# Top-k attention and an exact-GELU MLP on one core: more of P transposed by the vector engine and DRAM, with single buffers elsewhere to make room

## The chip, the cores and the metric

The kernel runs on one core of one Trainium2 chip, as one launch. The metric is the device time of the kernel in microseconds; lower is better. The engines are named as in the profile: PE (matmuls and transposes through the array; PEld is its weight loads), DVE (vector), ACT (scalar, activations), POOL (general) and SP, which only issues DMAs here. Each engine executes its own instructions strictly in the order of the program; what ties engines together are waits on semaphores.

## The reference

```python
B, H, S, D = 8, 8, 576, 64                       # q, k, v: (B, H, S, D)
scores = matmul(q, k.T) / sqrt(D)
kth = 32nd largest of each row
scores = where(scores >= kth, scores, -1e9)
attn = exp(scores - max); attn /= attn.sum(-1) + 1e-9
x = matmul(attn, v)  ->  (B * S, H * D) = (4608, 512)
h = x @ w_in                                      # (512, 2048)
out = (0.5 * h * (1 + erf(h / sqrt(2)))) @ w_out  # (2048, 512)
```

All is float32.

## The kernel before

**Items.** Two heads of a batch are a pair, four pairs a batch. The 576 rows of a head are 4 times 128 (`NM`, main rows) and 64 last rows. An item is a tile of scores of 128 partitions by 2 x 576: a main item has 128 rows of both heads of a pair, a last item the 64 last rows of the four heads of two pairs. There are 144 items, 18 to a batch; an even batch has its two last items behind the main ones, an odd batch ahead of them, so that four last items stand together (16 to 19, 52 to 55, 88 to 91, 124 to 127). 36 items, two batches, are a period of everything that follows.

**Slots.** One pass of the main loop is called slot n here. It is a software pipeline written out by hand: the loop issues, in this order and to every engine's queue, the work of slot n, and nothing reorders it later. In slot n:

- scores of item n+2 (in even slots also of n+3) are made by PE and copied by ACT into a tile `s` (L386, L394; `bufs=6`);
- the P of item n-2 is transposed, because the product with v needs the keys on the partitions (`transposes`). Either PE does it, with eight transposes into `tp` (L649), one or two of the 64 keys at the end (`tp_t`, L619, L622), and ACT copies them to `pt` (L664, L629, for last items `pt_end`, L635); or the item is *squared*: DVE transposes all 32x32 squares of `s` (`square_p`, L569), SP writes it to DRAM (`write_p`, L579, four DMAs) and reads it back into `pt` with the squares in their places (`read_p`, L586, four DMAs, one slot later). Before the change the squared items are 48 even main items from item 28 on;
- the product of P and v (`attend`, L715; last items L726) is made for item n-3, for main items once for two of them; ACT copies it into `xT`;
- select (Prelu against the 32nd value, L517) and exp (L529) of item n-1 run on ACT; the sum of exp goes to POOL (`add_small`, L510), the reciprocal to DVE (`inverse`, L504), and POOL multiplies the tile by it (`normalise`, L552);
- the top 32 of item n are found on DVE by MAX8 and MATCH_REPLACE8 (`top_k`, L483, L486), first on the pairwise maxima of the two halves of a row, whose sums POOL makes and splits (`sum_up` L447, `smaller` L455). `top_k` calls `middle` (the square of item n-2) ahead of its third round and `last` (the reciprocal of item n-1) at its end. `threshold` (L497, L498, POOL) then gives select its operands;
- pieces of the MLP fill PE (`mlp`, with a fixed number per slot from `room_in`).

**The MLP** goes by blocks of 256 tokens. In even slots PE makes pieces of the first product (`h_ps`, L773), which ACT passes through Gelu (L789) at the start of the odd slot; in odd slots it makes the second product in a form with seven products for eight (`second_block`): `seven_piece` (L927) and six `trio_piece`s (L929) that accumulate in three banks. In order of its pieces, an odd slot is one last piece of h, `seven`, then the others. A block takes four such odd slots. The first `seven` of a block is copied by ACT into a tile `y7` (L945), those of the other three are copied to `p7` (L948) and added to it by POOL (L950). When a block ends, ACT copies the banks out and POOL makes the four quarters of y from them: five sums (L979 to L983), then `lower` (L990), the last reader of `y7`, and `upper` (L994). POOL's sums are put in a list, `small`, from which `run_small` takes a few at the end of each slot, behind `normalise` and `sum_up`. Between blocks lie, once in a ring of 1152 tokens, 128 last tokens in a plainer form (`even_piece`); the very first block is plain too.

**PSUM** has eight banks: three for the second product, two each under the tags `pr` (scores, `tp`) and `l1` (h; in even slots also the second scores), and one, `z`, that the key scores (`last_keys`, `t_ps` or `tp_t`), the tails, `seven` and the product `o` take in turns. Whoever writes `z` next must wait until ACT has copied out what stands there.

**DMA.** SP issues nearly all of them in order. `load` brings q and k of a later pair for DVE to transpose by squares, with eight DMAs for each (four of 512 rows, four of the 64 last rows); calls that go through `issue` are held back in slots whose item n-2 is squared, until that item's write is issued.

## Time and profile before

| | |
|---|---|
| runs of the kernel before | 1480.89, 1480.30, 1479.78 us; median 1480.3 |
| the profiled execution, its own time | 1479.73 us |
| span of its instructions | 1478.0 us |
| busy, share of the span | PE 99%, DVE 88%, POOL 77%, ACT 74% |
| DMA, mean | 76 GB/s; queue q1 35.3% of 16 engines |

The span runs from the first to the last instruction that was profiled; the time of the execution has 1.7 us around it. In a row of a group stand the line, the engine, the operation, the tiles (out<-in), partitions and elements, the count, and then the busy time in us, the mean of one in ns, and the idle time ahead of it with what ended it. In a row of a timeline stand the start and the length in us, then the same names with the count of equal instructions merged. A float32 product shows as two rows of matmul for one instruction of the program, a transpose as one. Names drop the numbers of buffers, so `y` in `y<-seven` is the tile `y7`.

### The profile page before, as it was taken

Reading aid. Unit: us, or ns where it says so; the run is one execution under the profiler, and the core shown is the slowest. Engines: PE = TensorE matmul, PEld = TensorE weight load, DVE = VectorE, ACT = ScalarE, POOL = GpSimd, SP = SyncE. Lnnn points to the kernel's source line nnn. Section 1 sums busy time; section 2 is a strip of 40 time slices with the busy share of each in tenths; the row PEclk is TensorE's granted clock in tenths of the full one; section 3 lists DMA queues with packets and bytes.
Section 4 is the critical chain, followed back from the end, with each engine's and each line's share of the span. In section 5 each row is a group of like instructions: output and inputs, shape, how many; then the busy total and the mean of one; then the engine's idle time right before and its main releaser. Section 6 shows DMA issues by size and latency. Waiting matters only on the chain. (4 is left out here: it accounts for less than half of the span.)

```text
span 1478.0 us, 27006 instructions
## 1 busy us (share of the span) xinstructions
PE 1461.6 (99%) x8817; PEld 1147.9 (78%) x8817; DVE 1294.3 (88%) x3318; ACT 1099.9 (74%) x1942; POOL 1140.1 (77%) x1291
## 2 busy tenths in 40 slices
PE   8999999999999999999999999999999999999999
PEld 6876677877777777887777778787777777787787
DVE  8999899999999988999999987999999997998701
ACT  7999977877777687777777778777777777776620
POOL 6877567877898879877898978886788887987732
PEclk9999999999999999999999999999999999999999
DMA  7424310045435322345534331345453421233300
GB/s 198 143 86 124 84 48 1 24 88 101 95 73 93 66 58 52 65 95 108 105 83 81 69 61 47 66 93 99 97 103 73 89 55 41 61 61 72 70 15 15
DMA packets 477645, 112.94 MB, mean 76 GB/s; under 512 B 413216, under 2 KB 469056, under 8 KB 477504
## 3 DMA queue, kind: packets, MB, share of 16 engines
q1 hardware_dynamic: 476240, 110.78, 35.3%
q8 instruction: 70, 1.15, 0.3%
q14 instruction: 71, 0.58, 0.1%
q10 hardware_dynamic: 1200, 0.39, 0.1%
q0 software_dynamic: 64, 0.03, 0.0%
HBM read 73.39 MB, written 37.75 MB: 75 GB/s over the span
## 5 line engine op out<-in xcount | busy, mean ns | idle before, releaser
L773 PE MATMUL h_ps<-xT,w_in_sb 128*128 128x256 f32 (+1 forms) x2560 | 536.2, 361 | 0.1
L773 PEld LDWEIGHTS h_ps<-xT,w_in_sb 128*128 128x128 f32 x2560 | 436.5, 190 | 73.4 <-issue 25.2
L483 DVE MAX8 top<-lists 128x8 f32<-128x576 f32 (+1 forms) x792 | 476.4, 641 | 0.0
L486 DVE MATCH_REPLACE8 lists<-top,lists 128x288 f32<-128x288 f32 (+1 forms) x528 | 307.9, 589 | 0.0
L552 POOL TENSOR_TENSOR s<-s,rden 128x1152 f32<-128x1152 f32 x135 | 285.8, 2117 | 0.3 <-DVE rden L504 0.3
L529 ACT ACTIVATE s<-s,bias 128x576 f32<-128x576 f32 x288 | 225.4, 787 | 11.0 <-issue 0.4
L517 ACT ACTIVATE s<-s,neg 128x576 f32<-128x576 f32 x288 | 225.5, 793 | 1.7 <-POOL neg L497 1.6
L510 POOL TENSOR_SCALAR den<-den 128x2 f32<-128x2 f32 x144 | 31.4, 218 | 215.9 <-ACT s L529 210.2
L455 POOL TENSOR_TENSOR lists<-lists 128x576 int32<-128x576 int32 x132 | 186.2, 1410 | 4.0
L447 POOL TENSOR_TENSOR lists<-s 128x576 int32<-128x576 int32 x133 | 187.2, 1407 | 0.0
L715 PE MATMUL o<-pt,raw_v 128*64 128x256 f32 x1280 | 153.0, 384 | 1.8 <-ACT s L529 1.1
L715 PEld LDWEIGHTS o<-pt,raw_v 128*64 128x64 f32 x1280 | 87.8, 136 | 85.8 <-issue 37.2
L789 ACT ACTIVATE g<-h_ps 128x512 f32<-128x512 f32 x144 | 78.2, 594 | 100.6 <-PE h_ps L773 100.4
L929 PE MATMUL y_ps<-w_out_sb,sum 128*128 128x256 f32 x472 | 140.4, 379 | 0.0
L394 ACT ACTIVATE s<-s_ps 128x1024 f32<-128x1024 f32 x127 | 125.5, 1035 | 10.5 <-PE s_ps L386 10.3
L664 ACT COPY pt<-tp 128x1024 f32<-128x1024 f32 x85 | 86.6, 1019 | 62.2 <-PE tp L649 62.1
L386 PE MATMUL s_ps<-kt,qm 64*128 64x512 f32 x512 | 129.4, 618 | 0.8 <-ACT s L392 0.8
L504 DVE RECIPROCAL rden<-den 128x2 f32<-128x2 f32 x144 | 23.2, 161 | 108.6 <-POOL den L510 107.4
L486 DVE MATCH_REPLACE8 lists<-first,lists 128x288 f32<-128x288 f32 x264 | 114.3, 439 | 0.0
L929 PE MATMUL y_ps<-w_out_sb,g 128*128 128x256 f32 x480 | 113.4, 379 | 0.0
L483 DVE MAX8 first<-lists 128x8 f32<-128x288 f32 x268 | 106.6, 436 | 0.0
L929 PEld LDWEIGHTS y_ps<-w_out_sb,g 128*128 128x128 f32 x480 | 91.2, 190 | 12.4
(167 smaller groups left out, 2533.1 us busy)
## 6 DMA issues: line engine op xcount, KB each, us to landing
turned<-s SPq DMA_DIRECT2D x192, 144.0 KB, 3.5
pt<-turned SPq DMA_DIRECT2D x192, 144.0 KB, 3.2
raw_v<-in_v_dram SPq DMA_DIRECT2D x64, 128.0 KB, 2.4
out_dram<-y SPq DMA_DIRECT2D x30, 256.0 KB, 2.1
raw_q<-in_q_dram SPq DMA_DIRECT2D x112, 64.0 KB, 2.0
raw_k<-in_k_dram SPq DMA_DIRECT2D x112, 64.0 KB, 2.0
w_out_sb<-in_moe_w_in_dram SPq DMA_DIRECT2D x14, 511.8 KB, 4.8
w_out_sb<-in_moe_w_out_dram SPq DMA_DIRECT2D x10, 511.8 KB, 4.1
```

The costliest lines, as they stand in the source:

```text
L386: nc.tensor.matmul(s_ps[:, e], lhsT=q_t[rows, :], rhs=kt[rows, 0:SM], start=True, stop=True)
L394: nc.scalar.activation(spread(s, S + TL, SM), s_ps, func=AF.Copy, scale=scale)
L447: nc.gpsimd.tensor_tensor(t[:, :, 1].bitcast(i32), a.bitcast(i32), b.bitcast(i32), op=ALU.add)
L455: nc.gpsimd.tensor_tensor(into_of(i)[:, :, 1].bitcast(i32), both, top, op=ALU.subtract)
L483: nc.vector.max(x[:, e], src[:, e])
L486: nc.vector.match_replace(dst[:, e], x[:, e], src[:, e], LOWEST)
L517: nc.scalar.activation(s, s, func=AF.Prelu, bias=st["neg"][:, e : e + 1], scale=1.0, alpha=STEEP)
L529: nc.scalar.activation(s, s, func=AF.Exp, bias=st["bias"][:, e : e + 1], scale=1.0, accum_out=st["den"][:, e : e + 1],)
L552: nc.gpsimd.tensor_tensor(s, s, wide, op=ALU.mult)
L715: nc.tensor.matmul(o[e * D : (e + 1) * D, 0:n], lhsT=vt[:, j, e, :], rhs=pt[:, e * NJ + j if j < NM else NM, :], start=(j == 0), stop=(j = ...
L773: nc.tensor.matmul(h_tile(u)[:, i, :], lhsT=w_in_sb[:, ko, f * P : (f + 1) * P], rhs=xT[:, ko, c0 : c0 + n], start=(ko == 0), stop=(ko == ...
L929: nc.tensor.matmul(acc[names][:, k], lhsT=lhsT, rhs=rhs, start=(j == 0 and k == 0), stop=(j == FT // 2 - 1 and k == 1),)
```

## The change

- `squared` also holds for last items (from item 52 on) and for odd main items whose number in the period is 3, 13, 21, 25 or 29. Four last and five odd items of a period are added: 28 in all, 12 and 16.
- The last items get the layout of main items (keys of the second head turned round), so that they are squared and read into `pt` like those; `pt_end` goes.
- For the added odd items (`later`) the chain is moved forward: in the slot after theirs the reciprocal is taken ahead of the very last MAX8 (`early`) and `normalise` stands ahead of `threshold` on POOL; in the next the square follows the first MAX8s (`late`). Their product moves to the end of slot n+3. The products of delayed last items move too (`mid`: behind `seven` in an odd slot), and two MLP pieces move from a slot to the next where that next slot has no product at its usual place (`bare`).
- q and k of a pair come with four DMAs each, not eight, and through `issue`. The small loads of v behind delayed last items go to ACT's queue.
- Room in SBUF: seven tiles `s` instead of six; `part` has two buffers instead of three, `y7` one instead of two; p5 is kept in the half of `y1` that it ends in, and the sum is made in place.

```diff
-                    for at, lo, hi, by in ((0, 0, SM, queue), (SM + e * TL, SM, S, queue2)):
-                        by.dma_start(
...
+                    queue.dma_start(
+                        out=t[rows, at : at + S].rearrange("i (c j) -> i c j", j=SQ),
+                        in_=src[b, h0 + e, :, cols].rearrange("(c i) j -> i c j", i=SQ),
+                    )
...
-                load("q", pair + ahead)
+                issue(lambda: load("q", pair + ahead))
...
-        S_of[i] = s = work.tile([P, 2 * S], f32, tag="s", bufs=6, name="s")
+        S_of[i] = s = work.tile([P, 2 * S], f32, tag="s", bufs=7, name="s")
...
-    def top_k(i, last, middle):
+    def top_k(i, last, middle, early, late):
...
-            if 16 * r == TOPK:
+            if 16 * r == TOPK and not late:
                 middle()
             for e in range(2):
                 nc.vector.max(x[:, e], src[:, e])
+                if early and e == 0 and r == len(rounds) - 1:
+                    last()
+            if r == 0 and late:
+                middle()
...
-            if r == len(rounds) - 1:
+            if r == len(rounds) - 1 and not early:
                 last()
...
-        return SINGLE.stop - 2 < i < N - 2 and i % 2 == 0 and items[i][1] < NM and i % RINGS != 12
+        if not SINGLE.stop - 2 < i < N - 2:
+            return False
+        return items[i][1] == NM or (i % RINGS in LATER if i % 2 else i % RINGS != 12)
+
+    def later(i):
+
+        return i % 2 == 1 and squared(i) and items[i][1] < NM
+
+    def delayed(i):
+
+        return squared(i) and items[i][1] == NM
...
+    LATER = (3, 13, 21, 25, 29)
...
-                issue(lambda r=r: load("v", pair + r + NP))
+                issue(lambda r=r: load("v", pair + r + NP, None, nc.scalar if delayed(i) else None))
...
-        return work.tile([P, HALF], f32, tag="part", bufs=3, name="part")
+        return work.tile([P, HALF], f32, tag="part", bufs=2, name="part")
...
-            y7[0] = work.tile([P, HALF], f32, tag="y7", bufs=2, name="y7")
+            y7[0] = work.tile([P, HALF], f32, tag="y7", bufs=1, name="y7")
             nc.scalar.copy(out=y7[0], in_=seven[0][:, 0:HALF])
...
-            p2, p5, s7 = end_of["p2"], part_tile(), y7[0]
+            p2, p5, s7 = end_of["p2"], y1[:, B2], y7[0]
...
-            small.append((1, lambda: pool(y1[:, B2], s7, p5, op=add)))
             small.append((1, lambda: pool(y0[:, B2], y0[:, B2], p5, op=add)))
+            small.append((1, lambda: pool(p5, s7, p5, op=add)))
...
+    def bare(n):
+
+        return (n - 4 in starts and delayed(n - 4)) or later(n - 3)
...
-        return sizes[x] + (1 if x % 2 == 0 else -1)
+        return sizes[x] + (1 if x % 2 == 0 else -1) + 2 * (bare(n) - bare(n + 1))
...
-        read_p(n - 3)
+        mid = [i for i in (n - 5, n - 4) if delayed(i) and n % 2 and (i % 2 or i in starts)]
+        if not mid:
+            read_p(n - 3)
...
-        product = attend(n - 3)
+        if delayed(n - 4) and n % 2 == 0 and n - 4 not in starts:
+            product = attend(n - 4)
+        else:
+            product = not delayed(n - 3) and not later(n - 3) and attend(n - 3)
...
             softmax(n - 1, 0)
+            if mid:
+                for i in mid:
+                    attend(i)
+                copy_x()
+                read_p(n - 3)
             if n % 2:
                 mlp(ODD)
...
         run_gelus()
+        if later(n - 3):
+            attend(n - 3)
+            copy_x()
         if n < N:
-            top_k(n, lambda: inverse(n - 1), lambda: square_p(n - 2))
+            top_k(
+                n, lambda: inverse(n - 1), lambda: square_p(n - 2), later(n - 1), later(n - 2)
+            )
...
+        if later(n - 1):
+            normalise(n - 1)
         threshold(n)
...
-        normalise(n - 1)
+        if not later(n - 1):
+            normalise(n - 1)
```

## The prediction, as put on record before the changed kernel was run

> **What bounds the kernel now.** I read the page's head first, then the busy time by stretch, then the groups of the engine that fills its stretch.

> ```profile
> span 1478.0 us, 27006 instructions
> PE 1461.6 (99%) x8817; PEld 1147.9 (78%) x8817; DVE 1294.3 (88%) x3318; ACT 1099.9 (74%) x1942; POOL 1140.1 (77%) x1291
> ...
> core 0: us, PE busy (x) PEld busy (x) DVE busy (x) ACT busy (x) POOL busy (x), PEclk, DMA share, GB/s
> ...
> 703.60:1051.70 348.10, 347.59 (x2085) 273.54 (x2083) 321.92 (x832) 262.85 (x470) 286.62 (x323) 1.00 0.40 79
> ```

> The last row is one whole period of the schedule, two batches or 36 items (the window runs from the first MAX8 of item 72 to that of item 108). PE has work in 347.59 of its 348.10 us, DVE in 321.92. Busy PE alone would prove little, so I looked at the pace: the chain of waits shows runs of transposes and of products at a steady rate.

> ```profile
> 1279.34 0.87 PE tp L649 x8
> 1280.21 1.73 PE y_ps L929 x8
> ```

> Eight transposes take 0.87 us (0.109 each), eight passes of 256 columns 1.73 (0.216 each), one behind the other with no time between. So PE's own work sets the time: a microsecond of work less there is a microsecond less, and a microsecond in which PE waits is a microsecond more, because nothing after it has slack to make it up.

> **What the change takes away.**

> ```profile
> L649 PE MATMUL tp<-ident,s 128*128 128x128 f32 x696 | 90.4, 273 | 0.0
> L619 PE MATMUL tp_t<-ident,s 128*128 128x128 f32 x71 | 20.5, 288 | 1.6 <-POOL s L552 1.2
> L622 PE MATMUL tp_t<-ident,s 128*64 128x128 f32 x32 | 6.1, 273 | 0.0
> L664 ACT COPY pt<-tp 128x1024 f32<-128x1024 f32 x85 | 86.6, 1019 | 62.2 <-PE tp L649 62.1
> L569 DVE STREAM_TRANSPOSE s<-s 128x1152 f32<-128x1152 f32 x48 | 65.5, 1364 | 0.0
> ```

> The new `squared` holds 76 items where it held 48: 12 of the 16 last-row items and 16 odd main ones. These 28 lose eight transposes each, 28 x 0.87 = 24.4 us. Of the tails 16 (of L619) and 32 (L622) go and 4 come, 44 x 0.109 = 4.8. PE sheds 29.2 us, all of it on the path.

> DVE gains 28 x 1.364 = 38.2 us, nine squares or 12.3 us in a period: 321.92 + 12.3 = 334.2, against a PE period of 348.1 less 9.4 (nine items of 29.2 / 28), 338.7. DVE stays under PE, so I cost the squares at nothing; if the fit fails, the rival below prices it. ACT sheds 28 x 1.019 us of copies and takes 24 small loads of v onto its queue, which by a quarter of the read row below (2.54 / 4 = 0.64) are 15 us; ACT is busy in 262.85 of 348.10, so nothing. The halved q and k loads (4 DMAs, not 8) now stand behind a write in SP's queue; they only matter to DVE's transposes of q and k, in the same slack. The seventh tile of scores and the two `part` tiles meet no wait that I can find. The in-place sums swap an output, not an operation.

> **The moved chain.** An odd item's P must now be normalised, squared, written, read back, and used at the end of the next slot but one.

> ```profile
> 592.35 3.26 SPq L579 DMA_DIRECT2D turned<-s  x4
> 598.47 2.54 SPq L586 DMA_DIRECT2D pt<-turned  x4
> ...
> pt<-turned SPq DMA_DIRECT2D x192, 144.0 KB, 3.2
> ```

> From the first write to the first read is 6.1 us, the fourth read is issued 1.9 later and lands after 3.2: 11.3 us from the square. The square stands about 3 us into its slot, the product at the end of the next, some 16 us after the slot's start (two slots of 348.1 / 36 = 9.7 us, less the work behind it and PE's lead over DVE): 2 us to spare, less where a read of the neighbour stands ahead on SP. Putting `normalise` (2.10 us, below) ahead of `threshold` on POOL also delays the next item's select by up to that. Both together: 0 to 0.5 us for each of 16 items, 0 to 8; I take 2, near the lower end, since the spare is positive.

> In the period's slot 59 the products of items 54 and 55 stand directly behind `seven` and need the same bank z, which ACT must first empty. Slot 57's rows, further down, show this copy ending 1.1 us after `seven`: three times 1.1 = 3.3 us.

> **What the room costs.** `y7` goes from two buffers to one. Its first write of a token block is ACT's copy of `seven` (L945); its last read is POOL's `lower` (L990). This is a handover between two blocks, in slot 77 (the row of `tp` shows that its item is still transposed there; the other handovers of a period have the same queues):

> ```profile
> 740.74 2.10 POOL L552 TENSOR_TENSOR s<-s,rden 128x1152 f32<-128x1152 f32 x1
> 748.42 1.40 POOL L455 TENSOR_TENSOR lists<-lists 128x576 int32<-128x576 int32 x1
> 749.90 0.22 POOL L510 TENSOR_SCALAR den<-den 128x2 f32<-128x2 f32 x1
> 751.01 2.10 POOL L552 TENSOR_TENSOR s<-s,rden 128x1152 f32<-128x1152 f32 x1
> 753.07 1.40 POOL L447 TENSOR_TENSOR lists<-s 128x576 int32<-128x576 int32 x1
> 754.45 0.72 POOL L980 TENSOR_TENSOR y<-y,y 128x256 f32<-128x256 f32 x1
> ...
> 757.20 0.72 POOL L990 TENSOR_TENSOR y<-y,y 128x256 f32<-128x256 f32 x1
> ...
> 750.98 0.38 ACT L945 COPY y<-seven 128x256 f32<-128x256 f32 x1
> ...
> 754.33 0.25 ACT L629 COPY pt<-tp_t 128x128 f32<-128x128 f32 x1
> 755.53 1.01 ACT L664 COPY pt<-tp 128x1024 f32<-128x1024 f32 x1 [0.95 <-PE tp L649]
> ...
> 758.39 1.94 ACT L394 ACTIVATE s<-s_ps 128x1024 f32<-128x1024 f32 x2 [0.27 <-PE s_ps L386]
> ...
> 749.81 1.03 PE L927 MATMUL seven<-w_sum,g 128*128 128x256 f32 x4
> 750.67 1.89 PE L929 MATMUL y_ps<-w_out_sb,g 128*128 128x256 f32 x8
> ...
> 753.26 0.38 PE L349 MATMUL tp_t<-kt,qm 128*128 128x128 f32 x2
> ...
> 757.16 1.99 PE L386 MATMUL s_ps<-kt,qm 64*128 64x512 f32 x8
> 759.07 2.38 PE L715 MATMUL o<-pt,raw_v 128*64 128x256 f32 x20
> ```

> The copy starts at 750.98; `lower` ends at 757.92. With two buffers the one did not wait for the other; with one it must, 6.9 us, and in the changed program's order ACT's copy does carry a wait for POOL's `lower`. POOL cannot be earlier: from 740.74 on its rows follow each other without a gap, and the sums stand in its queue behind two `normalise` and the lists. What queues behind the copy is all of ACT: the select and exp of the next item, the copies of `tp` and of the scores. Bank z stays full, and the next PE instruction that uses z (`tp_t`, 753.26) starts at 757.92 + 0.38 = 758.3 instead. PE, in order, stands still for 5.0 us.

> Then ACT is 6.9 late and PE only 5.0. Where the slot still has a transposed item (slots 49, 85, 121), the scores need the bank of `tp`: ACT reaches the end of that copy 5.2 us after the `seven` copy (756.54 - 751.36), less its wait of 0.95, so at 762.5; PE comes at 757.16 + 5.0 = 762.2. Another 0.3 to 0.4: 5.4 us. Where the item is now squared (41, 77, 113), no product follows and h comes 0.22 + 0.86 + 1.92 + 1.73 us after z is free, at 763.0, but needs the scores copied: 9.0 us after the `seven` copy before (760.33), less the copies that went (0.25, 1.01) and two waits (0.95, 0.27), 6.5, so 764.8. Another 1.8: 6.8 us. The third kind (57, 93, 129) has item 53's product right behind `seven`:

> ```profile
> 560.30 0.81 PE L927 MATMUL seven<-w_sum,g 128*128 128x256 f32 x3
> ...
> 561.81 0.38 ACT L945 COPY y<-seven 128x256 f32<-128x256 f32 x1
> ...
> 566.37 0.72 POOL L990 TENSOR_TENSOR y<-y,y 128x256 f32<-128x256 f32 x1
> ```

> `seven` ends at 561.11, the copy would end at 567.09 + 0.38 = 567.5: 6.4 us. Of the 15 L945 copies nine are such handovers; five follow a block of even or plain pieces, and the last stands in the tail, where POOL is ahead. Sum: 3 x (5.4 + 6.8 + 6.4) = 55.8 us. Bounds: 9 x 4.0 = 36, if POOL's part of the chain comes a microsecond or so earlier, and 9 x 6.9 = 62.

> **The clock.**

> ```profile
> 1474.40:1478.00 3.60, 0.00 (x0) 0.00 (x0) 0.78 (x3) 0.00 (x0) 0.00 (x0) 0.87 0.31 109
> ...
> 1.04 4.21 PE L1113 MATMUL warm<-raw_v 128*128 128x128 f32 x18 [1.04 <-DVE raw_v L85]
> ...
> L1113 PE MATMUL warm<-ident 128*128 128x128 f32 x276 | 32.7, 275 | 0.0
> ```

> In the last 3.6 us PE has no instruction and the mean granted clock is 0.87: a fall to one half some 2.7 us after PE stopped. Coming from rest PE runs slowly: 18 matmuls in 4.21 us, 0.23 each, where later ones take 32.7 / 276 = 0.12. One fall thus costs about 4.21 - 18 x 0.118 = 2.1 us. PE now stands for 5.0 us and more nine times, so a fall can come nine times, 0 to 18.9 us; I take it at the three longest, 6.3, since no row shows a stop of 5 us amid work.

> [...]

> **The sum**, against the profiled execution's own 1479.7 us (0.6 under the runs' median of 1480.3): 1479.7 - 29.2 + 55.8 + 3.3 + 2 + 6.3 = 1517.9, say 1518.

> **Rivals.**
> 1. *The handover does not decide, and the kernel is faster.* It needs `lower` to be done by about the time that z is wanted: the wait must shrink from 6.9 to under 2 us. For it: POOL is idle a fifth of the period. Against: not here, where its rows touch. Break-even with the 29.2 us is 3.2 us of PE standstill for each of nine. Time: 1479.7 - 29.2 + 3.3 + 2 = 1456, or 1465 if DVE, with 4.5 us to spare a period, also holds PE up by 3 us in each of three. Chance 0.08.
> 2. *Every stop lets the clock fall.* The same sum with 18.9 instead of 6.3: 1530, or 1537 with waits at their 6.9. For it: the fall after 2.7 us. Against: the second wait of slots 41, 77 and 113 would hide part of it. Chance 0.30.
> 3. *The waits are shorter than read* (36 us, no fall): 1479.7 - 29.2 + 36 + 3.3 + 2 = 1492; a little less and it is a draw. For it: a standstill also lets POOL catch up before the next handover. Against: eight slots lie between, and the chain is rebuilt in each. Chance 0.10, with 0.02 more for a draw.
> 4. *PE's transposes were not the limit*, so nothing comes back for 29.2 us: 1547. The pace of PE's rows speaks against it. Chance 0.03.

> **How the numbers follow.** The forecast's own case has 0.47. A measurement of this kernel can tell about 0.2%, 3 us, from no change. Faster: 0.08. Within: 0.02. Slower: 0.90. The range runs from 1487 (a bit under rival 3) to 1541 (rival 2 with its upper bounds); left out are rivals 1 and 4, the draw, and the outer edges.

> **What would show it.** In the waits of the changed profile: ACT's copy `y<-seven` waiting for POOL's `y` about nine times, some 60 us together; PE waiting for that copy in the key scores or products that follow, about 5 us each; a period of about 360 us (348.1 - 9.4 + 18.6 + 1.1 and the small terms); PE's busy share clearly under 99%; the granted clock below 1.00 in the slices with handovers, if it falls. Right even if the sum is wrong: `tp` x472 at 0.109 us, 76 squares at 1.36. I am wrong if `y<-seven` shows no wait for POOL, or PE's period shrinks to 339.

## The result, and the profile after

The changed kernel takes 1600.3 us (median of four runs, 1599.3 to 1601.2) where the kernel before takes 1480.2 (four runs, 1479.8 to 1480.9): 1.081 times as long, 95% interval 1.079 to 1.083. Forecast were 1518, 1487 to 1541. The sign was right; of the 120 us only 38 were foreseen.

The head of the page after:

```profile
span 1599.3 us, 26413 instructions
...
PE 1473.8 (92%) x8549; PEld 1145.5 (72%) x8549; DVE 1351.1 (84%) x3347; ACT 1064.9 (67%) x1867; POOL 1142.8 (71%) x1290
```

And the same whole period as in the prediction, from the first MAX8 of item 72 to that of item 108, in the busy time by stretch (start:end, length, busy time of each engine, PEclk, DMA share, GB/s):

```profile
745.40:1135.50 390.10, 352.55 (x2000) 273.90 (x1998) 339.95 (x842) 251.84 (x447) 287.27 (x323) 0.96 0.50 98
```

A period has grown from 348.1 to 390.1 us, not to 360. PE stood idle in 0.5 us of it and now does in 37.5. And its busy time went up by 5 us although 85 instructions went: the clock column, 1.00 before, says 0.96. Over the whole span PE's idle time went from 16.4 to 125.5 us (span less busy), and its busy time from 1461.6 to 1473.8, where 1432.4 was due if 29.2 us of work went. These 29.2 did go: `tp` has 472 instructions for 696. So the account is -29.2 of work, +109.1 of standing still, +41.4 of work at a slower clock: +121.3, which is the difference of the spans.

Where PE stands still, by what ended the wait (the list of waits after: engine, line, waited for: us in total, times, the longest):

```profile
ACT y L971 <- POOL y L1015: 67.1, 9, 8.6
...
PE o L736 <- DMA pt<-turned: 29.0, 15, 4.7
PE o L747 <- ACT y L971: 29.0, 3, 9.7
...
PE o L747 <- DMA pt<-turned: 15.4, 3, 5.6
PE tp_t L367 <- ACT y L971: 15.1, 3, 5.0
PE t_ps L367 <- ACT y L971: 14.9, 3, 5.1
```

The rows with ACT's `y` are the handover of `y7`, nine times, as forecast: ACT's copy of the first `seven` waits for POOL's `lower`, and PE waits for ACT, 29.0 + 15.1 + 14.9 = 59.0 us. The two rows `pt<-turned` are products that wait for a squared P to come back from DRAM: 44.4 us, where the kernel before had none and the prediction allowed 2 for them and the later select together.

The rest of this document asks three things. Is the handover really worth what its rows say? What makes the products wait? And why does the slow clock cost 41 us where 6 were set down?

### The profile page after: what moved, and what is told of

Read it like the earlier page. It is cut to its first block, busy times and chain, and to the rows that moved or that the text cites. A ratio compares the mean times of both kernels' runs of the same rounds, so it can differ in the third digit from the quotient of the medians.

```text
span 1599.3 us, 26413 instructions
## 1 busy us (share of the span) xinstructions
PE 1473.8 (92%) x8549; PEld 1145.5 (72%) x8549; DVE 1351.1 (84%) x3347; ACT 1064.9 (67%) x1867; POOL 1142.8 (71%) x1290
## 5 line engine op out<-in xcount | busy, mean ns | idle before, releaser
L736 PE MATMUL o<-pt,raw_v 128*64 128x256 f32 x1280 | 158.3, 394 | 31.4 <-DMA pt<-turned 29.0
L736 PEld LDWEIGHTS o<-pt,raw_v 128*64 128x64 f32 x1280 | 94.0, 139 | 106.7 <-issue 61.3
L955 PE MATMUL y_ps<-w_out_sb,sum 128*128 128x256 f32 x472 | 143.2, 386 | 0.0
L402 PE MATMUL s_ps<-kt,qm 64*128 64x512 f32 x512 | 133.7, 637 | 0.8 <-ACT s L408 0.8
L437 DVE TENSOR_TENSOR lists<-s 128x576 f32<-128x576 f32 x133 | 122.8, 924 | 0.6
L741 ACT COPY xT<-o 128x256 f32<-128x256 f32 x64 | 24.9, 389 | 144.7 <-PE o L736 144.7
L516 POOL TENSOR_SCALAR neg<-top 128x2 f32<-128x2 f32 x144 | 67.7, 470 | 74.8 <-DVE rden L523 62.6
L955 PE MATMUL y_ps<-w_out_sb,g 128*128 128x256 f32 x480 | 121.1, 398 | 0.0
## 6 DMA issues: line engine op xcount, KB each, us to landing
turned<-s SPq DMA_DIRECT2D x304, 144.0 KB, 3.5
pt<-turned SPq DMA_DIRECT2D x304, 144.0 KB, 3.2
```

The lines of the kernel that those rows point to most:

```text
L402: nc.tensor.matmul(s_ps[:, e], lhsT=q_t[rows, :], rhs=kt[rows, main_keys(pair)], start=True, stop=True)
L736: nc.tensor.matmul(o[e * D : (e + 1) * D, 0:n], lhsT=vt[:, j, e, :], rhs=pt[:, e * NJ + j if j < NM else NM, :], start=(j == 0), stop=(j = ...
L955: nc.tensor.matmul(acc[names][:, k], lhsT=lhsT, rhs=rhs, start=(j == 0 and k == 0), stop=(j == FT // 2 - 1 and k == 1),)
```

## Experiments

Two theories went into the first four runs. Theory 1: the handover of `y7` and what hangs on it is most of the loss. Theory 2: it is the added squares with their trips through DRAM. All times are medians; the kernel before ran beside each at 1480.0 to 1480.4.

| kernel | us | against before |
|---|---|---|
| changed kernel | 1600.3 | +120.1 |
| before, one `y7` (`b_y7one`) | 1540.1 | +59.9 |
| changed, matmuls in the nine waits (`a_awake`) | 1581.7 | +101.6 |
| changed, first `seven` by way of p7 (`a_p7`) | 1536.7 | +56.6 |
| p7, last rows only (`a_p7_last`) | 1503.7 | +23.5 |
| p7, odd items only (`a_p7_odd`) | 1528.1 | +47.9 |
| p7, older P read (`a_p7_stale`) | 1530.6 | +50.4 |
| p7, q and k loads at once (`a_p7_now`) | 1528.1 | +47.9 |
| the same, last rows only (`a_p7_last_now`) | 1494.6 | +14.4 |
| p7, q and k loads on ACT's queue (`a_p7_act`) | 1627.1 | +147.1 |
| the same, older P read (`a_p7_act_stale`) | 1627.5 | +147.5 |
| last rows, v loads on ACT's queue (`a_p7_last_now_v`) | 1512.7 | +32.7 |
| last rows, q, k, v loads on ACT's queue (`a_p7_last_act_v`) | 1635.9 | +155.9 |
| p7, without q and k loads (`a_p7_noqk`) | 1517.9 | +37.6 |
| the same, older P read (`a_p7_noqk_stale`) | 1507.5 | +27.1 |
| last rows, without v loads (`a_p7_last_nov`) | 1476.3 | -4.0 |
| p7, six last rows and item 25 (`a_p7_half25`) | 1492.6 | +12.3 |
| p7, no added square (`a_p7_base`) | 1480.4 | 0.0 |
| two `y7`, item 25 alone (`a_25`) | 1483.6 | +3.2 |

### The handover alone, and taken away

`b_y7one`, an edit of the kernel before:

```diff
-            y7[0] = work.tile([P, HALF], f32, tag="y7", bufs=2, name="y7")
+            y7[0] = work.tile([P, HALF], f32, tag="y7", bufs=1, name="y7")
```

> The kernel before with one change: y7 has one buffer instead of two; no square, no write and read of P, no other DMA is added. Theory 1 (the handover of y7 carries most of the loss): TensorE stops nine times as in the changed kernel, six times about 5.0 us and three times about 4 us (there it still has the transposed work that the changed kernel lost), 42 us together, 3 us of knock-on waits and about 25 us of half clock behind the nine stops: about 1550 us. Theory 2 (the added squares and their trips through DRAM carry most of it): under 1495 us.

It took 1540.1. PE's line of its page, and two of its waits:

```profile
PE 1482.5 (96%) x8817; PEld 1162.9 (76%) x8817; DVE 1294.3 (84%) x3318; ACT 1100.2 (71%) x1942; POOL 1141.2 (74%) x1291
```

```profile
ACT y L945 <- POOL y L990: 56.6, 9, 6.9
...
PE tp_t L349 <- ACT y L945: 41.1, 9, 5.0
```

PE does the same work as before (8817 instructions) and stands still 41.1 us for the copy; its busy time is 1482.5 instead of 1461.6, 20.9 more for the same instructions, with nine stretches of half clock in the trace. 62.1 was the prediction's price for handover and clock together, and 59.9 is measured. That the two agree is luck: the stops are shorter here (41.1 for 55.8, since PE still has the transposes of the added items) and the clock costs more (20.9 for 6.3).

`a_p7` takes the handover out of the changed kernel: the first `seven` goes into the tile that the other three use, and POOL, behind its own `lower`, copies it over.

```diff
-            y7[0] = work.tile([P, HALF], f32, tag="y7", bufs=1, name="y7")
-            nc.scalar.copy(out=y7[0], in_=seven[0][:, 0:HALF])
+            t = work.tile([P, HALF], f32, tag="p7", bufs=1, name="p7")
+            nc.scalar.copy(out=t, in_=seven[0][:, 0:HALF])
+
+            def take():
+                y7[0] = work.tile([P, HALF], f32, tag="y7", bufs=1, name="y7")
+                nc.gpsimd.tensor_scalar(y7[0], t, 1.0, None, op0=ALU.mult)
+
+            small.append((1, take))
...
-        into = y7[0]
-        small.insert(0, (1, lambda: nc.gpsimd.tensor_tensor(into, into, t, op=ALU.add)))
+        small.insert(0, (1, lambda: nc.gpsimd.tensor_tensor(y7[0], y7[0], t, op=ALU.add)))
```

> The changed kernel, but the first seven-tile reduction of a block is written by ScalarE into the second pair tile p7 instead of y7, and GpSimd copies it to y7 behind its own lower(): ScalarE waits for nothing of GpSimd any more; squares, trips through DRAM and q/k loads stay. Theory 1: the nine stops (59 us), their half clock (about 35 us) and the knock-on waits in slots 59, 95 and 131 go: 1480 to 1506 us. Theory 2 (squares and trips through DRAM): 1560 us or more.

It took 1536.7: 63.6 less than the changed kernel, which again is the handover's price, but far from the 1480 to 1506 of theory 1. So both theories were half right. The handover is half of the loss, and another 56.6 us, with 29.2 us less work for PE, were still there. Most of them are the trips. PE stands still 65.3 us more than in the kernel before, and 55.7 of this are the two rows `pt<-turned` (39.9 and 15.8; they were 29.0 and 15.4, so the stops at the handover seem to have hidden part). Its busy time is 1453.2, 20.8 over the 1432.4 that were due, at a mean clock of 0.986.

### The clock in the nine stops

`a_awake` leaves all waits and puts matmuls that nobody reads ahead of the instruction that waits.

```diff
+        if awake[0] and tag == "z":
+            warm = pair_tile("warm")
+            for _ in range(40 if name == "o" else 20):
+                nc.tensor.matmul(warm[:, 0, 0:P], lhsT=ident, rhs=ident, start=True, stop=True)
+            awake[0] = False
...
```

(The lines left out choose the nine places.)

> The changed kernel with matmuls that nobody reads (identity by identity) put on TensorE right ahead of the nine instructions that wait for ScalarE's y7 write: 20 at two of the three kinds of place, 40 at the third. The waits stay, only TensorE isn't idle in them. If the half clock behind the nine stops costs about half of the 75 us that it lasts: about 1565 us. If a fall costs the 2.1 us of the prediction: about 1580. If the clock plays no part: 1600.

It took 1581.7, 18.6 less. None of the nine stretches of half clock behind the handovers is left in its trace, so that is 2.1 us for each of nine stops, what the prediction charged for a fall. Three stretches of the changed kernel around the stop of slot 41, in the busy time by stretch, show what one is like.

```profile
405.00:412.13 7.13, 3.59 (x17) 2.83 (x15) 7.10 (x16) 1.08 (x2) 7.05 (x9) 1.00 0.46 108
412.14:418.96 6.82, 5.66 (x14) 2.79 (x14) 4.87 (x11) 5.92 (x10) 3.71 (x7) 0.50 0.66 147
418.97:423.00 4.03, 4.03 (x20) 3.37 (x19) 4.03 (x14) 3.21 (x6) 4.03 (x4) 1.00 0.49 141
```

PE stops at 408.6. The clock is halved from 412.1, when the stop is nearly over, and PE's 5.66 us of work there would have taken about half, by an estimate from the same trace: products of 256 columns (L955) start 0.45 us apart in its stretches of half clock and 0.22 elsewhere. The trace has 16 such stretches in the changed kernel ahead of the tail: nine behind the handovers and seven behind products that waited for DRAM.

### Which trips

`a_p7_last` has no odd later item, `a_p7_odd` no last rows:

```diff
-    LATER = (3, 13, 21, 25, 29)
+    LATER = ()
```

```diff
-        return items[i][1] == NM or (i % RINGS in LATER if i % 2 else i % RINGS != 12)
+        return items[i][1] < NM and (i % RINGS in LATER if i % 2 else i % RINGS != 12)
```

> The previous p7 kernel with no odd later item squared (only the last rows' P go by squares and DRAM, the later items' P is transposed by TensorE as before). If the trips of the odd later items are the rest of the loss: 1465 to 1475 us, under the kernel before, since TensorE sheds some 13 us and waits no more. If the rest has another cause (the last rows' own trips, the q/k loads, VectorE): within 5 us of the p7 kernel.

> The p7 kernel with the last rows' P transposed by TensorE as in the kernel before; only the 16 odd later items are squared in addition. If the two groups of trips add up: 1480 + (1537 - 1504) = 1513 us. If they only hurt each other by meeting in SyncE's queue: under 1490 us.

Neither was as expected: 1503.7, not 1465 to 1475, and 1528.1, not 1513. Each group alone loses to the kernel before, the odd items more, and together they cost less than the sum (56.6 against 23.5 + 47.9), perhaps because a wait for one also gives the other time; no run shows that.

`a_p7_base` keeps layout, room, the p7 copy and the four loads (issued at once) and adds no square.

```diff
-        return items[i][1] == NM or (i % RINGS in LATER if i % 2 else i % RINGS != 12)
+        return items[i][1] < NM and (i % RINGS in LATER if i % 2 else i % RINGS != 12)
-    LATER = (3, 13, 21, 25, 29)
+    LATER = ()
```

> The changed kernel's layout, room and q and k loads (four, issued at once), the p7 copy, and no added square: the 48 items of the kernel before. If layout and room cost nothing by themselves, all of the loss is the y7 wait and the trips: 1477 to 1481 us. If the short waits under 0.8 us that every variant shows (6 to 10 us more than the kernel before) come from the layout: 1485 to 1490.

1480.4, a ratio of 1.0001 (0.9992 to 1.001): the layout, the room and the halved loads together cost nothing. The place of the loads behind a write is not in this kernel; it comes next.

### Why the products wait: the odd items

Three suspects: loads that stand ahead of the read in SP's queue (theory B below), the landing of the own write, and PE being too early (together theory A: the trip is too long by itself; A2 is its later form). First, the loads of q and k back to where the kernel before has them (at once, not behind the write):

```diff
-                issue(lambda: load("q", pair + ahead))
+                load("q", pair + ahead)
```

(and the same for k.)

> The p7 kernel, with the q and k loads issued at once where the kernel before had them, not held back until behind the write (so that they no longer stand between an item's write and its read). If this order is what makes the reads late: reads start 6.1 us behind the square instead of up to 9, the waits of slots 32, 37, 52, 68 and 74 and their like (about 25 us with the clock) mostly go: 1505 to 1515 us. If not: 1530 to 1540 us, or more if the loads now hold up the writes.

> The previous one without odd later items (last rows only, q and k loads at once). The waits of slots 34, 37, 70, 74, 106 and 109 (9.6 us) go if the order of the loads made them: about 1492 us. The waits of slots 56 and 59 and their like (3 x 5 us and their clock, 6 us) stay by that theory, since v loads and out stores stand there. If the order plays no part: 1500 to 1505 us.

With last rows only, 9.0 us went (1494.6, expected 1492), and with them the waits of slots 34, 37, 70, 74, 106 and 109: these were even items, squared before the change too, whose reads the reordered loads had made late. With the odd items as well only 8.6 went (1528.1, of two runs at 1525.1 and 1531.1; expected 1505 to 1515): there the loads now hold up the write instead. In slot 88 it starts 3.4 us behind the square (875.17 for 871.76), and the wait was even 6.9 us.

`a_p7_stale` lets each read take the tile of three squared items before, so that it doesn't wait for its own write.

```diff
...
             d = turned.pop(i)
+            older_d.append(d)
+            d = older_d[-4:][0]
...
```

> The p7 kernel, but each read of a squared P takes from DRAM the tile that was written three squared items earlier (eight buffers there instead of two), so that no read waits for its own write to land; squares, writes, reads and loads are as many as before, and the products work on older P. Theory A (the length of the trip through DRAM, from the square to the landed read, is what TensorE waits for): the 56 us of product waits on the read mostly go, and the 15 us that the half clock costs with them: 1460 to 1480 us. Theory B (it is the place in SyncE's queue: q, k and v loads and other trips ahead of the read, not the landing of the own write): the reads still come late; over 1510 us.

1530.6, six less. That spoke for the queue (theory B), but told nothing of the worst waits, slots 52, 88 and 124: in all of them the read stood behind loads anyhow. Putting the loads on ACT's queue was to part the two:

```diff
-                issue(lambda: load("q", pair + ahead))
+                issue(lambda: load("q", pair + ahead, nc.scalar if pair >= SQUARES else None))
```

(and the same for k.)

> The p7 kernel with the q and k loads of the later pairs on ScalarE's queue instead of SyncE's, at the same place in the program. Theory A2 (the trip of an odd item is too long by itself, 12.4 us from the end of the square to the product even with nothing ahead of the read, while TensorE stands ready some 9 us behind the square): the waits of slots 52, 88 and 124 shrink from 5.0 to 6.0 us to about 3.5, and those of 32, 37, 68, 74 and 78 by 1 to 2 us: 1510 to 1520 us. Theory B (the q and k loads ahead of the read make all of the wait): those waits go altogether, below 1505 us. If ScalarE's own work is what is now late: above 1530.

> Both at once: q and k loads on ScalarE's queue, and each read takes the tile written three squared items earlier, so that it waits neither for a load in the queue nor for its own write to land. Theory A2: the trip is now its issues alone, some 9.5 us, about what TensorE leaves it: waits of the odd items under 1 us, only the last rows' waits of slots 59, 95 and 131 stay: 1480 to 1495 us. If neither the landing nor the queue is what makes the product late: as the kernel without the older tiles, within 5 us.

Both took 1627 us and decided nothing. The loads now take ACT's own time, and everything of ACT queues behind them. Its 216 loads of q and k in `a_p7_act` took 115 us to issue, 0.53 each, and before many of them ACT waits until DVE has done with the old q or k. It stands still for 168 us at 38 places with such issues, 97 of them issuing. The list of waits of `a_p7_act`, for its next instruction, the table load of Gelu:

```profile
ACT L815 <- DVE top L498: 63.5, 11, 7.2
...
ACT L815 <- DMA raw_q<-in_q_dram: 24.2, 4, 6.8
```

So the loads were left out, not moved.

```diff
-            ahead = 1 if pair >= SQUARES else 2
+            if pair >= SQUARES:
+                return
+            ahead = 2
```

> The p7 kernel without the q and k loads of the later pairs (VectorE's transposes of them run all the same, on the q and k that are there). SyncE's queue then has no load between an odd item's write and its read. Theory A2 (the trip by itself is too long): the read starts 6.1 us behind the square everywhere, the product at 12.4 at the earliest; the waits of slots 52, 88 and 124 go from 5.1, 6.0, 5.9 to about 3.5, those of slots 32, 37, 68, 74 and 78 to under 1; the last rows' waits stay: 1505 to 1515 us. Theory B (the loads make the wait): the waits of slots 52, 88 and 124 go under 1 us too: 1485 to 1500.

> The previous one, with each read taking the tile written three squared items earlier, so that it doesn't wait for its own write to land. Theory A2: the trip is 2.6 us shorter, 9.8 us from the square to the product, and the waits of slots 52, 88 and 124 go under 1 us, 8 to 12 us less than the previous kernel with their clock: 1495 to 1503. Theory B: within 3 us of the previous kernel.

1517.9 and 1507.5. The timeline of the trip for the product in slot 88 (item 85), first in `a_p7`: SP's write, loads and read, PE's last work ahead of the product, and the product.

```profile
877.63 3.36 SPq L610 DMA_DIRECT2D turned<-s  x4
881.03 2.90 SPq L124 DMA_DIRECT2D raw_k<-in_k_dram  x4
883.98 2.12 SPq L124 DMA_DIRECT2D raw_q<-in_q_dram  x4
886.20 2.54 SPq L620 DMA_DIRECT2D pt<-turned  x4
...
881.04 5.45 PE L799 MATMUL h_ps<-xT,w_in_sb 128*128 128x256 f32 x24
892.46 4.11 PE L736 MATMUL o<-pt,raw_v 128*64 128x256 f32 x18 [5.98 <-DMA pt<-turned]
```

Without the loads (`a_p7_noqk`):

```profile
865.66 3.36 SPq L612 DMA_DIRECT2D turned<-s  x4
871.85 2.54 SPq L622 DMA_DIRECT2D pt<-turned  x4
...
868.99 5.45 PE L801 MATMUL h_ps<-xT,w_in_sb 128*128 128x256 f32 x24
877.08 4.06 PE L738 MATMUL o<-pt,raw_v 128*64 128x256 f32 x20 [2.64 <-DMA pt<-turned]
```

And with an older P as well (`a_p7_noqk_stale`):

```profile
862.94 3.27 SPq L613 DMA_DIRECT2D turned<-s  x4
866.32 3.17 SPq L625 DMA_DIRECT2D pt<-turned  x4
...
866.26 5.45 PE L804 MATMUL h_ps<-xT,w_in_sb 128*128 128x256 f32 x24
872.28 1.08 PE L741 MATMUL o<-pt,raw_v 128*64 128x256 f32 x8 [0.57 <-ACT s L388]
```

The write is issued within 0.1 us of the square's end. Counted from its start, PE is ready for the product after 8.9, 8.8 and 8.8 us, always the same. The product starts after 14.8, 11.4 and 9.3. So the loads make 3.4 us of the 6.0, and the landing of the own write about all of the other 2.6: with nothing in the queue the trip still takes 11.4 us, and PE leaves it 8.8. In slots 52, 88 and 124 together the waits are 17.0 us in `a_p7`, 8.9 without the loads (2.5, 2.6 and 3.8) and 2.5 with an older P as well. Theory A2 is right that the trip is too long by itself (it expected 3.5 us of wait each), and theory B's loads are worth about half. Both kernels came out 3 to 5 us above what A2 expected in all, which leads to the next point.

### What is left when the trip is short enough

`a_p7_noqk_stale` no longer waits for odd trips to speak of (1.5 us at most), and is still 27 us over the kernel before. PE's longest waits in it:

```profile
PE tp_t L657 <- POOL s L573: 15.0, 13, 2.1
PE o L752 <- DMA pt<-turned: 13.0, 4, 4.3
PE o L741 <- DMA pt<-turned: 4.8, 4, 1.5
```

and its busy time in a stretch 3 us longer than a period (358.4):

```profile
713.70:1075.00 361.30, 346.01 (x2015) 268.73 (x2010) 342.35 (x853) 253.91 (x450) 294.21 (x329) 0.99 0.46 93
```

DVE is busy in 342.35 us of it, where 321.92 were in a period before. Of the waits, the second is the last rows', below. The first is new: PE waits for `normalise` of items that it transposes itself. One row of the groups, in the kernel before and then in the changed kernel, shows what came over DVE and POOL:

```profile
L422 DVE TENSOR_TENSOR lists<-s 128x576 f32<-128x576 f32 x133 | 100.8, 758 | 0.0
```

```profile
L437 DVE TENSOR_TENSOR lists<-s 128x576 f32<-128x576 f32 x133 | 122.8, 924 | 0.6
```

The mean of DVE's pairwise maxima rose from 758 to 924 ns. By the single instructions sixteen take 2.1 us, one for each odd item, one near the start takes 1.2, and the others 0.76. The sixteen lie under the `normalise` that was moved ahead of `threshold`. In `a_p7`, at the turn from slot 86 to 87, DVE's rows and then POOL's:

```profile
871.73 0.17 DVE L523 RECIPROCAL rden<-den 128x2 f32<-128x2 f32 x1 [1.70 <-POOL den L529]
871.82 0.74 DVE L498 MAX8 top<-lists 128x8 f32<-128x576 f32 x1
872.59 2.11 DVE L437 TENSOR_TENSOR lists<-s 128x576 f32<-128x576 f32 x1
...
871.98 2.11 POOL L571 TENSOR_TENSOR s<-s,rden 128x1152 f32<-128x1152 f32 x1 [0.28 <-DVE rden L523]
```

POOL's multiplication runs from 871.98 to 874.09; DVE's maxima, with 0.76 us of work, begin at 872.59 and end at 874.70, 0.6 us after POOL's. The reciprocal ahead of the last MAX8 waited another 1.7 us for POOL's `den`. So moving the chain forward costs DVE 1.35 us and a wait, and there are five such items in a period. The trace of the changed kernel has the same for all of its sixteen odd items: DVE's maxima (L437) begin 0.60 to 0.61 us behind POOL's multiplication, end 0.61 to 0.62 behind its end, and take 2.11 to 2.12 us, where 116 others take 0.74 to 0.76.

`a_25` is the test of that, with nothing else in the way: two `y7`, and the one odd item whose product had not waited.

```diff
-        return items[i][1] == NM or (i % RINGS in LATER if i % 2 else i % RINGS != 12)
+        return items[i][1] < NM and (i % RINGS in LATER if i % 2 else i % RINGS != 12)
-    LATER = (3, 13, 21, 25, 29)
+    LATER = (25,)
-            y7[0] = work.tile([P, HALF], f32, tag="y7", bufs=1, name="y7")
+            y7[0] = work.tile([P, HALF], f32, tag="y7", bufs=2, name="y7")
```

(score tiles back to six, q and k loads at once.)

> The changed layout with two buffers of y7, six tiles of scores, q and k loads at once, the last rows' P transposed as before, and one odd item in a period squared (25 of 36; four in all, less those outside the range). TensorE sheds 3 or 4 x 0.98 us: 1475 to 1478 us if the product doesn't wait, 0.2 to 0.3% faster than the kernel before. If it waits by 1 us like the others: 1480.

1483.6, a ratio of 1.0021 (1.0012 to 1.003). One product waits for a trip, by 0.5 us, three `tp` groups went, and it is slower by 3 us. In slot 62, the one ahead of its square, `a_25` has

```profile
614.95 0.17 DVE L523 RECIPROCAL rden<-den 128x2 f32<-128x2 f32 x1 [0.91 <-POOL den L529]
...
615.80 2.11 DVE L437 TENSOR_TENSOR lists<-s 128x576 f32<-128x576 f32 x1
```

and that slot takes 11.7 us on DVE, 9.6 in `a_p7_base`. The same 2.1 us lie in slots 98 and 134. PE loses its time at just these places. Between the `seven` of 615.7 us and the next one at 675.7 it stops twice, 1.9 us in all, where `a_p7_base` has no stop, and the same holds one and two periods later (1.8 us each; in the last, 0.5 is the wait for the trip). The longer of the two waits for the `normalise` of the next item:

```profile
639.97 0.33 PE L652 MATMUL tp_t<-ident,s 128*128 128x128 f32 x1 [1.34 <-POOL s L571]
```

So an odd item loses even when its trip is in time: the stops exceed the 0.98 us of transposes that it saves. That `normalise` is late because of DVE's 2.1 us is argued from these rows; no run takes that alone away.

### Why the products wait: the last rows

In `a_p7_last_now` one wait is left in each period, that of slots 59, 95 and 131, 3.6 to 4.1 us (and a single one of 1.3). SP's queue ahead of slot 95's:

```profile
905.27 3.41 SPq L610 DMA_DIRECT2D turned<-s  x4
908.78 6.63 SPq L134 DMA_DIRECT2D raw_v<-in_v_dram  x4
915.68 2.61 SPq L620 DMA_DIRECT2D pt<-turned  x4
918.40 3.35 SPq L610 DMA_DIRECT2D turned<-s  x4
921.80 2.95 SPq L134 DMA_DIRECT2D raw_v<-in_v_dram  x4
924.85 0.92 SPq L870 DMA_DIRECT2D out_dram<-y  x2
925.86 2.61 SPq L620 DMA_DIRECT2D pt<-turned  x4
```

Four last items follow each other, each with a write and a read, and the loads of v for the next batch stand between. Moved to ACT's queue:

```diff
-                issue(lambda r=r: load("v", pair + r + NP, None, nc.scalar if delayed(i) else None))
+                issue(lambda r=r: load("v", pair + r + NP, nc.scalar if delayed(i) else None))
```

> Last rows only, q and k loads at once, and the large v loads behind a last row's product on ScalarE's queue (where the small ones are already) instead of SyncE's. If the v loads (6.6 and 3.0 us of SyncE's queue between the trips of three items that follow each other) make the waits of slots 59, 95 and 131: these go, with their half clock: 1474 to 1480 us. If it is the trips themselves (three in three slots, 9.7 us each): 1490 to 1495.

> Last rows only, with q, k and v loads all on ScalarE's queue at the places of the changed kernel (behind the write), so that SyncE has nothing but trips and stores. If only SyncE's queue counts: as the last one or up to 3 us under it, 1471 to 1480. If ScalarE's queue is now the late one: above 1485.

1512.7 and 1635.9, both worse. With the v loads alone ACT waits for no tile; the issuing itself is what it pays. At six places it issues eight loads in 4.6 to 4.9 us, and its next instruction comes 3.8 to 4.1 us late. The last two of eight, and that instruction:

```profile
914.15 0.60 ACTq L134 DMA_DIRECT2D raw_v<-in_v_dram  x1
914.79 0.72 ACTq L138 DMA_DIRECT2D raw_v<-in_v_dram  x1
915.54 1.28 ACT L815 ACT_TABLE_LOAD   x1 [3.92 <-DMA raw_v<-in_v_dram]
```

With q and k on ACT's queue too, the waits of `a_p7_act` come on top. Left out instead (`range(0 if delayed(i) else ...)` around that call):

> Last rows only, q and k loads at once, without the v loads (large and small) behind a last row's product. If these loads' place in SyncE's queue makes the waits of slots 59, 95 and 131 (3.6 to 4.1 us each and their half clock): they go, 1474 to 1479 us, under the kernel before. If three trips in three slots are too many by themselves: 1490 to 1495.

1476.3, a ratio of 0.9977 (0.9967 to 0.9987), and no wait for a trip is left. So the v loads made the last rows' waits. It is also the most that the last rows could give, and this kernel doesn't load all of v: 4 us.

`a_p7_half25`, made from `a_p7_last_now`, with the trips that fit by all this:

```diff
-        return items[i][1] == NM or (i % RINGS in LATER if i % 2 else i % RINGS != 12)
+        if items[i][1] == NM:
+            return i % RINGS in (18, 19)
+        return i % RINGS in LATER if i % 2 else i % RINGS != 12
-    LATER = ()
+    LATER = (25,)
```

> A version made of what fits: the p7 copy, q and k loads at once, only the last rows of the second batch of a pair of batches squared (items 18 and 19 of 36; six of the twelve), and of the odd later items only item 25 of 36, whose product never waited. TensorE sheds 6 x 0.98 + 3 or 4 x 0.87 us, about 9 to 10 us; if no product waits: 1470 to 1474 us, faster than before. If one wait of 2 us or more stays in a period, or SyncE's queue is late with the v loads that now come earlier: 1476 to 1485.

1492.6. No product waits for DRAM, but `seven` of slots 58, 94 and 130 waits for POOL's sums, a wait that the kernel before doesn't have, with a fall of the clock behind each:

```profile
PE seven L955 <- POOL g L840: 8.5, 3, 2.9
```

No kernel that computes everything beat the one before.

## Why the prediction was right or wrong

- **What bounds the kernel: right.** PE had no slack, and each stop came out as time.
- **Work removed, 29.2: right.** `tp` lost 224 instructions, and every loss above adds up only with it.
- **The handover, 55.8: right in mechanism, and in its sum with some luck** (59.0; 41.1 alone in `b_y7one`), since two kinds came out shorter and the third longer. By kind: slots 49, 85 and 121 5.0 for 5.4; slots 41, 77 and 113 4.7 to 5.1 for 6.8, since the scores ran at half clock and hid the second wait, as rival 2 supposed; slots 57, 93 and 129 9.7 for 6.4, because PE reached them earlier: `seven` ends at 576.7, 2.1 us ahead of DVE's first MAX8 of the slot, where it ended 1.0 behind it before, and `lower` at 585.9, 7.1 behind it (7.0 before).
- **The clock, 6.3: mis-sized, above all for its count.** The price of one fall, 2.1, was about right (2.1 by `a_awake`, 20.9 / 9 = 2.3 by `b_y7one`). But all nine stops had one, which was rival 2 with 0.30, and so had seven waits for trips: 41.4 in all, 2.6 for each of 16. The windows of 3.41 us ahead of these 16 falls had PE busy for 0 to 36% (last section).
- **The moved chain, 2 with bounds 0 to 8: the step that failed.** 44.4 us of waits, and about half of the clock's loss behind them (41.4 less the 18.6 of `a_awake`). Three parts of it were wrong. The trip was taken as 11.3 us from the square (its terms give 11.2); it is 11.4 when nothing stands ahead of the read, but 14.8 in slot 88 of `a_p7`, since the q and k loads, costed at nothing because "they only matter to DVE", now stand between write and read. The time that PE leaves was taken as some 16 us from the slot's start; it is 11.0 in `a_p7` (886.5 less DVE's first MAX8 at 875.5): PE's lead over DVE was guessed and not read off. And the last rows' trips were given no term, though four of them and the v loads share SP's queue in five slots; the 3.3 for bank z behind `seven` was there, and 1.7 is measured (`PE o L747 <- ACT p L974`).
- **DVE stays under PE, costed at nothing: wrong.** 334.2 was expected in a period, 339.95 is measured, above the 338.7 left to PE. The squares are as forecast (76 of 1.362 us); the rest is the maxima that `normalise` now holds up. What this cost the changed kernel no run isolates; in `a_25` PE stops for 1.8 to 1.9 us per odd item.
- **Layout, loads and in-place sums at nothing: right** (`a_p7_base`) but for the loads' place in the queue, which was worth 8.6 us (`a_p7_now`) and 9.0 (`a_p7_last_now`).
- **The range** ended at 1541, rival 2 with the longest handover, because the trips stood in every case with 2 us; no rival priced them.

With the handover at 59.9 (`b_y7one`) and the rest at 56.6 (`a_p7`, after 29.2 us gained), the 120 us are found to within 4.

## What to carry to other kernels

A transfer that replaces an engine's work has two lengths: what it takes with everything that stands ahead of it in its queue, and what the consumer leaves it, which is the distance between producer and consumer on their own engines' timelines; read both off the trace before costing it at nothing (14.8 and 8.9 us in slot 88 of `a_p7`). A step that is moved forward moves onto whatever runs there now (0.76 us of DVE's became 2.11). And where a stop costs a slow clock, count the stops, all of them: the price of one is small (2.1 us by `a_awake`; there were 16).

## What the runs showed of the hardware that was not expected

```profile
321.35:324.76 3.41, 1.39 (x10) 0.90 (x10) 3.41 (x6) 0.00 (x0) 3.33 (x6) 1.00 0.93 181
324.76:328.17 3.41, 3.41 (x19) 1.89 (x15) 3.41 (x9) 0.00 (x0) 2.20 (x5) 0.50 0.93 142
...
782.15:785.56 3.41, 1.60 (x8) 1.07 (x6) 3.41 (x9) 2.10 (x6) 3.33 (x4) 1.00 0.54 143
785.56:788.97 3.41, 3.11 (x24) 2.33 (x25) 3.41 (x8) 0.68 (x2) 3.41 (x5) 1.00 0.67 101
```

- Where DVE's pairwise maxima and POOL's multiplication met, the one that began later took longer: DVE's 0.76 us became 2.11, sixteen times of sixteen in the changed kernel, and POOL's multiplication took 2.62 instead of 2.11 in the four places where it began under DVE's maxima (0.1 us behind their start), before and after the change.
- A DMA on ACT's queue cost ACT the time of its issue, 0.53 to 0.55 us each here, besides any wait for its destination, which stands in ACT's own order: +90 us for the q and k loads (115 us of issuing, `a_p7_act` against `a_p7`), +18 for the large v loads, which waited for no tile (`a_p7_last_now_v` against `a_p7_last_now`).
